# A hand-written list of moves reorders ScalarE, VectorE and GpSimd at the beginning of an attention and gMLP kernel

## The chip, the cores and the metric

The kernel runs as one program on one core of a Trainium2 chip. The core has five engines that each work through their own queue in order: TensorE (PE), VectorE (DVE), ScalarE (ACT), GpSimd (POOL) and SyncE (SP), which here only issues transfers. They wait for each other by semaphores. The metric is the device time of one execution in microseconds (us): 374.2 us, the median of three runs of the kernel before (373.38, 374.2 and 375.71).

## The reference

Two stages follow each other, all in float32. The first is chunked attention with memory: 4 batches, 8 heads, 768 tokens, head dimension 64; each chunk of 32 queries sees 8 memory slots and a window of its own 32 tokens, 16 before and 8 after. The second is a gated MLP with a spatial product.

```python
for c in range(nc):                      # 24 chunks of 32 queries
    k_full = concat([mem_k, k[l_start:r_end]]);  v_full = concat([mem_v, v[l_start:r_end]])
    scores = scale * q_c @ k_full.T
    a = exp(scores - max(scores));  a = a / (sum(a) + 1e-09)
    out[c] = a @ v_full
h = maximum(x @ w_in, 0);  u, v = h[..., :512], h[..., 512:]     # x: (4, 768, 512)
v_n = (v - mean(v)) / sqrt(var(v) + 1e-06)
v_s = einsum('ts,bsd->btd', w_spatial, v_n) + b_spatial
result = (u * v_s) @ w_out
```

## The kernel before, in words

**Tiling and stages.** Attention runs in 24 units of 128 queries (4 chunks of 32, all 8 heads). Each unit goes through: `prep` (ACT copies keys into `kmain`, L400), a burst of 32 small matmuls for the scores (L415, out `sx`), `softmax` (DVE: `top`, a maximum, L472; `sub`, subtract it, L476; ACT: `exp`, L481; DVE: `den`, sum, add, reciprocal, L486 to L489), `flip` (PE transposes the weights into `pt`, L503; ACT copies them to `pT`, L506), a second burst that multiplies by the values (L415, `sx<-vmain,pT`), `norm` (DVE, `xs`, L455), a transpose into `xt` (L519) and the copies to `x` (ACT L524, DVE L528). The values of unit i are written into the second half of the same PSUM tile `sx` that holds the scores of unit i+1. The product with `w_in` (L557 to L559) starts as soon as the first three units and pieces of `w_in` are ready, and is interleaved with the other units. Every float32 product of the second stage is three matmuls of two-part numbers, so each operand is first split.

**Pieces of w_in.** `w_in` arrives as float64 words in eight pieces (`big`, 512 KB each). `from_f64` turns a piece to float32: on ACT `scale_` (L861, into `st`) and `rest` (L866, in place in `big`), on DVE `shift` (two instructions, L870 and L871), on POOL `add` (L876). `split` then makes `high` on ACT (L890, `win_h`) and `low` on DVE or POOL (L894, `win_l`). The first piece is written win(0,1) here; its `low` is on POOL.

**Fillers.** `busy` (L255) gives PE 5, 4, 2, 29 and 1 matmuls on an identity (`idle`), each two records in the profile, between the first units. Nothing reads their result.

**What sets the order.** `Plan.op` collects operations with an engine, a modelled time, what they read and write, and a rank; `Plan.order` makes one list of all of them by modelled start times; `emit` runs through the list and records each operation's instructions. The order of the list is the order of every engine's queue. It also decides the waits: an instruction that touches a tile waits for those recorded ahead of it that wrote that tile, whichever half of the tile they wrote. Transfers on SP wait besides for an earlier transfer's landing (`transfer`), so that a bounded amount is under way.

**Operations that the change and the prediction speak of** (number in the plan, engine, line before): 17 ACT `rest` of win(0,1) L866; 15 ACT `scale_` of it L861; 16 DVE `shift` of it L870, L871; 18 POOL `add` of it L876; 19 ACT `high` of it L890; 20 POOL `low` of it L894; 94 ACT keys of unit 1 L400; 96 PE scores of unit 1; 90 and 100 ACT `exp` of units 0 and 1; 91 DVE `den` of unit 0; 98 and 99 DVE `top` and `sub` of unit 1; 92 and 102 PE transposes `pt` of units 0 and 1; 95 PE values of unit 0, written into unit 1's `sx`; 104 PE transpose `xt` of unit 0; 46 SP load of q for units 2 and 3.

Of the kernel before, what the change touches and what calls it, by code (L numbers as in the profile page):

```python
# [18 lines left out]
CH = 32  # L19
SLOT = 40  # L20
LEFT = 16
FIRST = ('a', 'b', 'w0', 'v0', 'w1', 'w2', 'w3', 'q1', 'v1', 'w4', 'v2', 'w5', 'w6', 'w7')
RANKS = (34.7, 9.5, 12.7, 26.3, 36.3, 2.9, 37.5, 38.2)
LOWS = ('POOL', 'DVE', 'DVE', 'DVE', 'POOL', 'DVE', 'DVE', 'POOL')
# [4 lines left out]
class Plan:  # L29
# [121 lines left out]
        return none  # L151

    def emit(self):
        for n in self.order():
            if n < 0:
                self.idle(-n)
            else:
                self.ops[n][2]()


@with_exitstack
def tile_chunked_attention_gmlp(
# [106 lines left out]
    def src(t, offset, ap):  # L269
        return bass.AP(tensor=t.tensor, offset=offset, ap=ap)  # L270
# [20 lines left out]
    def load(dst, src_, w, rank, r=(), eng="SP", slow=1.0, us=0.45, seq=False, drag=1.0, of=None):  # L291
        e = {"SP": nc.sync, "ACT": nc.scalar, "POOL": nc.gpsimd}[eng]
        n = 4
        for s in src_.shape:
            n *= s
        mb = n / 1e6 * slow
        n = op(eng, us, lambda: transfer(e, dst() if callable(dst) else dst, src_, mb, of), r=r, w=w, rank=rank, mb=mb,
               after=line.get(eng) if seq else None, drag=drag)
        if seq:
            line[eng] = n  # L300
# [10 lines left out]
    def spot(name, g, shape):  # L311
        if (name, g) not in t_:
            alloc(name, g, shape, F32)
        return t_[name, g]

    def load_qk(g, units=(0, 1), seq=True):
# [3 lines left out]
        nk = 2 * UT + CH  # L320
        lo = LEFT if c0 == 0 else 0
        hi = nk - LEFT if c0 + 2 * UC == NC else nk
        q0, q1 = units[0] * UT, units[-1] * UT + UT
# [5 lines left out]
        load(lambda: spot("k", g, [P, T, nk])[:, :, k0:k1],  # L329
             src(k, off - LEFT + k0, [[S, P], [P * S, T], [1, k1 - k0]]), w=[ks + (u,)], rank=10.0 * i, slow=1.15, seq=seq)  # L330

# [55 lines left out]
    def spread_mem(i, eng, rank):  # L387
        b, o = i // UB, (i % NV) * UC
        for r in range(2):
            rows = slice(r * D + CH, r * D + SLOT)  # L390

            def spread(rows=rows, r=r):
                to, of = vmain[rows, :, o:o + UC], memv[rows, b].unsqueeze(2).broadcast_to([M, T, UC, D])
                ins = {"DVE": nc.vector, "POOL": nc.gpsimd}[eng].tensor_copy(to, of)  # L394
                made.setdefault(("vmem", i % NV), []).append(ins.ins.name)
            op(eng, 1.1 if eng == "POOL" else 1.25, spread, r=[("memv", r)], w=[("vmem", i % NV, r)], rank=rank)
# [65 lines left out]
    def softmax(i, rank):  # L462
        c0 = (i % UB) * UC

        def top():
            s = t_["sx", i][:, :, 0]
            if c0 == 0:
                nc.vector.memset(s[0:CH, :, :, 0:LEFT], NEG)
            if c0 + UC == NC:
# [497 lines left out]
    for j in range(NV):  # L967
        spread_mem(j, "DVE" if j < 1 else "POOL", 1.0 + 10 * j)
    for x in FIRST:
        if x[0] == "w":  # L970
# [105 lines left out]
```

## Time and profile before

| what | value |
|---|---|
| median of three runs | 374.2 us |
| the profiled execution | 373.39 us, of which the span of the instructions is 371.6 us |
| PE busy | 356.2 us (96%) |
| DVE, ACT, POOL busy | 294.7, 186.9, 157.1 us |
| first matmul | 6.78 us |
| granted TensorE clock | 1.00 in every slice of the page |

Busy times are shares of the span; an engine's idle time is told with what ended it. A row of a timeline gives start, duration, engine, line and operation; what stands in brackets is the idle time of the engine before it and its releaser. Times are counted from the span's start. The profiled execution took 0.8 us less than the median of the runs.

### The profile page before, as it was taken

How to read it: one execution, taken by the hardware profiler on the slowest of the kernel's cores; microseconds unless marked ns; L12 is line 12 of the kernel's file. 1: busy time of each engine (PE TensorE's matmuls, PEld its weight loads, DVE VectorE, ACT ScalarE, POOL GpSimd, SP SyncE). 2: the span in 40 equal slices, each digit the busy share in tenths (PEclk: the TensorE clock that was granted, in tenths of full speed). 3: DMA queues.
4: the chain of work that ended last, by engine and by line, in shares of the span. 5: the costliest groups of instructions: out<-in, count | busy, mean ns of one | idle time of the engine just before them, and what ended most of it. 6: DMA issues, size and time to landing. Idle time of an engine off the chain costs nothing. (4 is left out here: it accounts for less than half of the span.)

```text
span 371.6 us, 11928 instructions
## 1 busy us (share of the span) xinstructions
PE 356.2 (96%) x5026; PEld 328.6 (88%) x5026; DVE 294.7 (79%) x480; ACT 186.9 (50%) x334; POOL 157.1 (42%) x154
## 2 busy tenths in 40 slices
PE   2899999999999999999999999999999999999995
PEld 2787888988889889889888899989999999999895
DVE  3799968669669499584797689999979896998894
ACT  3577553655555445544483445347434733744451
POOL 6254733366376057720024367851246025216400
PEclk9999999999999999999999999999999999999999
DMA  8998977885895894968743538204830572230015
GB/s 209 291 246 242 233 223 244 260 249 164 251 241 179 217 276 136 266 159 272 222 168 101 215 132 308 94 1 155 228 129 2 196 227 88 85 130 0 0 44 170
DMA packets 47557, 65.52 MB, mean 176 GB/s; under 512 B 4496, under 2 KB 38928, under 8 KB 47504
## 3 DMA queue, kind: packets, MB, share of 16 engines
q1 hardware_dynamic: 46848, 64.44, 58.1%
q8 instruction: 39, 0.64, 0.8%
q10 hardware_dynamic: 656, 0.33, 0.3%
q14 instruction: 14, 0.11, 0.1%
HBM read 45.88 MB, written 18.87 MB: 174 GB/s over the span
## 5 line engine op out<-in xcount | busy, mean ns | idle before, releaser
L707 PE MATMUL y<-wsp,op 128*128 128x384 f32 x288 | 52.4, 337 | 0.0
L761 POOL TENSOR_TENSOR ug<-st,ug 128x384 f32<-128x384 f32 x24 | 34.5, 1453 | 40.1 <-DVE st L753 35.6
L707 PEld LDWEIGHTS y<-wsp,op 128*128 128x128 f32 x288 | 49.9, 188 | 0.4 <-ACT st L747 0.3
L557 PE MATMUL f<-x,win_h 128*128 128x384 f32 x128 | 46.0, 359 | 0.2 <-issue 0.2
L559 PE MATMUL f<-x,win_h 128*128 128x384 f32 x128 | 43.2, 338 | 0.0
L558 PE MATMUL f<-x,win_l 128*128 128x384 f32 x128 | 43.2, 337 | 0.0
L557 PE MATMUL f<-win_h,x 128*128 128x512 f32 x96 | 41.1, 428 | 0.0
L707 PE MATMUL f<-wsp,op 128*128 128x384 f32 x216 | 39.7, 337 | 0.0
L687 DVE TENSOR_TENSOR op<-sm,op 128x768 fp32r<-128x768 f32 x32 | 36.6, 1144 | 2.0 <-ACT op L684 1.8
L558 PE MATMUL f<-win_h,x 128*128 128x512 f32 x96 | 37.9, 395 | 0.1
L707 PEld LDWEIGHTS f<-wsp,op 128*128 128x128 f32 x216 | 37.5, 188 | 0.3 <-DVE st L753 0.3
L559 PE MATMUL f<-win_l,x 128*128 128x512 f32 x96 | 37.7, 393 | 0.0
L707 PE MATMUL y<-wout,op 128*128 128x256 f32 x288 | 36.0, 281 | 0.9 <-DVE op L687 0.8
L455 DVE TENSOR_TENSOR xs<-sx,rec 128x512 f32<-128x512 f32 x24 | 16.6, 690 | 24.6 <-PE sx L415 24.4
L707 PEld LDWEIGHTS y<-wout,op 128*128 128x128 f32 x288 | 34.6, 188 | 1.6 <-DVE op L687 1.5
L593 POOL TENSOR_TENSOR rstd<-ve,mhalf 128x1 f32<-128x1 f32 x24 | 14.5, 604 | 49.0 <-DVE ve L589 47.1
L684 ACT CAST op<-sm 128x768 fp32r<-128x768 f32 x32 | 26.4, 836 | 16.5 <-DVE sm L670 16.4
L767 POOL TENSOR_TENSOR st<-st,bias 128x384 f32<-128x384 f32 x14 | 17.9, 1286 | 38.3 <-ACT st L747 28.7
L415 PEld LDWEIGHTS sx<-kmain,q 64*32 64x32 f32 x1536 | 17.3, 109 | 14.3 <-issue 12.9
L581 ACT ACTIVATE st<-f 128x512 f32<-128x512 f32 x24 | 14.4, 599 | 28.7 <-PE f L559 28.2
L415 PE MATMUL sx<-kmain,q 64*32 64x64 f32 x1536 | 21.3, 230 | 7.4 <-ACT kmain L400 6.8
L394 POOL COPY vmain<-memv 8x1024 f32<-8x1024 f32 x22 | 23.9, 1090 | 9.9 <-PE sx L415 7.7
(86 smaller groups left out, 780.9 us busy)
## 6 DMA issues: line engine op xcount, KB each, us to landing
vmain<-in_v_dram SPq DMA_DIRECT2D x48, 128.0 KB
u_far<-uo SPq DMA_DIRECT2D x32, 192.0 KB
vn_far<-st SPq DMA_DIRECT2D x24, 256.0 KB
vr<-vn_far SPq DMA_DIRECT2D x8, 768.0 KB
ug<-u_far SPq DMA_DIRECT2D x16, 384.0 KB
q<-in_q_dram SPq DMA_DIRECT2D x11, 512.0 KB
vmain<-in_v_dram SPq DMA_DIRECT2D x47, 96.0 KB
out_dram<-ot SPq DMA_DIRECT2D x33, 128.0 KB
```

The costliest lines, as they stand in the source:

```text
L394: ins = {"DVE": nc.vector, "POOL": nc.gpsimd}[eng].tensor_copy(to, of)
L415: ins = nc.tensor.matmul(o, w_, m, start=True, stop=True, skip_group_check=True)
L455: nc.vector.tensor_tensor(xs.rearrange("p t r d -> p r t d"), t_["sx", i][:, :, 1], rec.rearrange("p t r -> p r t").unsqueeze(3).broadcast ...
L557: nc.tensor.matmul(o, lh, rh, start=(j == 0), stop=False)
L558: nc.tensor.matmul(o, ll, rh, start=False, stop=False)
L559: nc.tensor.matmul(o, lh, rl, start=False, stop=(j == len(pairs) - 1))
L593: nc.gpsimd.tensor_tensor(a, t_["ve", i], mhalf, op=ALU.pow)
L684: nc.scalar.copy(half(0), of())
L687: nc.vector.tensor_tensor(half(1), of(), half(0).bitcast(F32), op=ALU.subtract)
L707: nc.tensor.matmul(o, x, y, start=first and m == 1, stop=m == 3 * chunks, skip_group_check=True)
L761: nc.gpsimd.tensor_tensor(g, t_[st(x)], g, op=ALU.mult)
L767: {"DVE": nc.vector, "POOL": nc.gpsimd}[eng].tensor_tensor(a, a, bias[:, 1], op=ALU.add)
```

## The change

A table of pairs (n, m) is applied to the plan's list: operation n is taken out and put right behind operation m. A second table says behind which PE operation how many fillers stand. The 48 pairs touch operations that run in the first 50 us. PE's queue and SP's queue come out with the same instructions in the same order as before, fillers included.

```diff
+MOVES = (
+    (17, 25), (19, 18), (98, 46), (91, 98), (99, 26), (100, 99), (97, 102), (103, 35), (101, 34), (105, 101),
+    ...
+)
+IDLES = ((87, 5), (92, 4), (95, 2), (104, 29), (132, 1))
...
     def emit(self):
-        for n in self.order():
-            if n < 0:
-                self.idle(-n)
-            else:
-                self.ops[n][2]()
+        order = [n for n in self.order() if n >= 0]
+        for n, m in MOVES:
+            order.remove(n)
+            order.insert(order.index(m) + 1, n)
+        idles = dict(IDLES)
+        for n in order:
+            self.ops[n][2]()
+            if n in idles:
+                self.idle(idles[n])
```

Lines behind the table stand 8 to 12 lower in the changed kernel (L400 becomes L412, L866 becomes L878).

**ScalarE, the first unit's part, before.** `p_228` and `p_323` are the weights of units 0 and 1, `big_169` and `st_266` the first piece of `w_in`:

```order
L400 COPY kmain0_147<-k_163 128x20x32
L400 COPY kmain1_148<-k_163 128x20x32
L481 ACTIVATE p_228<-p_228 128x512
L861 ACTIVATE st_266<-big_169 128x512
L866 ACTIVATE big_169<-big_169 128x512
L506 COPY pT_287<-pt_273 128x512
L481 ACTIVATE p_323<-p_323 128x512
L861 ACTIVATE st_333<-big_215 128x512
```

**ScalarE, the same place now** (`p_229`, `p_331`: units 0 and 1; `big_169`, `st_267`: the first piece):

```order
L412 COPY kmain0_147<-k_163 128x20x32
L878 ACTIVATE big_169<-big_169 128x512
L412 COPY kmain1_148<-k_163 128x20x32
L493 ACTIVATE p_229<-p_229 128x512
L873 ACTIVATE st_267<-big_169 128x512
L518 COPY pT_280<-pt_269 128x512
L902 CAST win_h_108<-st_267 128x512
L873 ACTIVATE st_329<-big_220 128x512
L493 ACTIVATE p_331<-p_331 128x512
```

The `rest` of the first piece now stands ahead of the keys of unit 1, and the `high` of the first piece ahead of the `exp` of unit 1.

**VectorE, from the `sub` of unit 0 to that of unit 1, before** (`sx_230`: scores of unit 1, later values of unit 0):

```order
L476 TENSOR_TENSOR p_228<-sx_182,mx_224 128x2x4x64
L486 TENSOR_REDUCE den_268<-p_228 128x8
L487 TENSOR_TENSOR den_268<-den_268,eps_103 128x8
L489 RECIPROCAL rec_271<-den_268 128x8
L472 TENSOR_REDUCE mx_285<-sx_230 128x8
L870 TENSOR_SCALAR st_266<-st_266 128x512
L871 SCALAR_TENSOR_TENSOR st_266<-big_169,st_266 128x512
L476 TENSOR_TENSOR p_323<-sx_230,mx_285 128x2x4x64
```

**VectorE, the same place now** (`sx_231`: the tile that was `sx_230`):

```order
L488 TENSOR_TENSOR p_229<-sx_182,mx_225 128x2x4x64
L882 TENSOR_SCALAR st_267<-st_267 128x512
L883 SCALAR_TENSOR_TENSOR st_267<-big_169,st_267 128x512
L484 TENSOR_REDUCE mx_322<-sx_231 128x8
L498 TENSOR_REDUCE den_324<-p_229 128x8
L499 TENSOR_TENSOR den_324<-den_324,eps_103 128x8
L501 RECIPROCAL rec_327<-den_324 128x8
L488 TENSOR_TENSOR p_331<-sx_231,mx_322 128x2x4x64
```

The same operations stand between the two `sub`; the `shift` comes first, then `top` of unit 1, then `den` of unit 0. In the list of all engines `top` of unit 1 (98) now stands behind operation 46, and so behind the burst 95 that writes into the tile it reads; before, it stood ahead of that burst.

**GpSimd, behind the four copies of memory values, before:**

```order
L876 TENSOR_TENSOR st_266<-st_266,big_169 128x512
L876 TENSOR_TENSOR st_333<-st_333,big_215 128x512
L876 TENSOR_TENSOR st_391<-st_391,big_264 128x512
L894 TENSOR_TENSOR win_l_109<-st_266,win_h_108 128x512
L876 TENSOR_TENSOR st_400<-st_400,big_278 128x512
```

**GpSimd, the same place now:**

```order
L888 TENSOR_TENSOR st_267<-st_267,big_169 128x512
L906 TENSOR_TENSOR win_l_109<-st_267,win_h_108 128x512
L888 TENSOR_TENSOR st_329<-st_329,big_220 128x512
L888 TENSOR_TENSOR st_381<-st_381,big_265 128x512
L888 TENSOR_TENSOR st_398<-st_398,big_278 128x512
```

The `low` of the first piece moved up from fourth to second place.

## Rows read from the trace of the kernel before

**Rows 1.** Waits of PE, 0 to 60 us: total us, times, longest.
```profile
PE sx L415 <- ACT kmain L400: 6.8, 1, 6.8
PE pt L503 <- ACT p L481: 0.9, 1, 0.9
PE pt L503 <- issue: 0.8, 1, 0.8
PE sx L415 <- issue: 0.6, 1, 0.6
```

**Rows 2.** Busy times by stretch: stretch, length, then PE, PEld, DVE, ACT, POOL.
```profile
49.00:371.60 322.60, 316.86 (x4199) 294.74 (x4199) 256.02 (x409) 157.12 (x283) 131.04 (x121) 1.00 0.53 166
```

**Rows 3.** Timeline of PE, 7 to 43 us.
```profile
7.88 2.50 PE L255 MATMUL idle<-ident 128*128 128x128 f32 x10
10.31 1.07 PE L415 MATMUL sx<-kmain,q 64*32 64x64 f32 x64
...
11.80 1.06 PE L255 MATMUL idle<-ident 128*128 128x128 f32 x8
12.79 0.86 PE L415 MATMUL sx<-vmain,pT 64*32 64x64 f32 x64
13.57 0.71 PE L255 MATMUL idle<-ident 128*128 128x128 f32 x4
15.18 0.44 PE L503 MATMUL pt<-ident,p 128*128 128x128 f32 x2 [0.89 <-ACT p L481]
16.37 0.38 PE L503 MATMUL pt<-ident,p 128*128 128x128 f32 x2 [0.75 <-issue]
...
17.02 6.64 PE L255 MATMUL idle<-ident 128*128 128x128 f32 x58
...
42.82 0.85 PE L415 MATMUL sx<-kmain,q 64*32 64x64 f32 x64
```

**Rows 4.** Waits of SP's queue, 7.6 to 10.2 us: total us, times, longest.
```profile
SPq L284 <- DMA big<-in_moe_w_in_dram: 2.2, 1, 2.2
```

**Rows 5.** Timeline of SP, 7.6 to 10.3 us.
```profile
9.79 0.35 SPq L284 DMA_DIRECT2D big<-in_moe_w_in_dram  x1
```

**Rows 6.** Timeline of ACT, 7 to 11 us.
```profile
7.92 0.73 ACT L400 COPY kmain<-k 128x640 f32<-128x640 f32 x1 [1.24 <-DMA k<-in_k_dram]
...
10.23 0.66 ACT L861 ACTIVATE st<-big 128x512 f32<-128x512 f32 x1
10.79 0.67 ACT L866 ACTIVATE big<-big 128x512 uint32<-128x512 uint32 x1
```

**Rows 7.** Timeline of DVE, 10 to 14 us.
```profile
10.35 0.69 DVE L486 TENSOR_REDUCE den<-p 128x8 f32<-128x512 f32 x1 [0.69 <-ACT p L481]
11.07 0.17 DVE L487 TENSOR_TENSOR den<-den,eps 128x8 f32<-128x8 f32 x1
...
11.46 0.69 DVE L472 TENSOR_REDUCE mx<-sx 128x8 f32<-128x512 f32 x1
12.07 0.42 DVE L870 TENSOR_SCALAR st<-st 128x512 uint32<-128x512 uint32 x1
12.52 0.69 DVE L871 SCALAR_TENSOR_TENSOR st<-big,st 128x512 uint32<-128x512 uint32 x1
13.71 0.69 DVE L476 TENSOR_TENSOR p<-sx,mx 128x512 f32<-128x512 f32 x1 [0.49 <-PE sx L415]
```

**Rows 8.** Timeline of POOL, 12 to 40 us.
```profile
13.46 1.28 POOL L876 TENSOR_TENSOR st<-st,big 128x512 uint32<-128x512 uint32 x1 [3.87 <-DVE st L871]
...
37.91 1.31 POOL L876 TENSOR_TENSOR st<-st,big 128x512 uint32<-128x512 uint32 x1 [1.66 <-ACT big L866]
```

**Rows 9.** Timeline of DVE, 38 to 43 us.
```profile
38.41 0.84 DVE L487 TENSOR_TENSOR den<-den,eps 128x8 f32<-128x8 f32 x1
...
42.03 0.68 DVE L455 TENSOR_TENSOR xs<-sx,rec 128x512 f32<-128x512 f32 x1
```

**Rows 10.** Busy times, from the `sub` of unit 1 to the `norm` of unit 3.
```profile
13.71:42.03 28.32, 26.08 (x459) 22.35 (x460) 25.89 (x45) 21.14 (x37) 13.94 (x13) 1.00 0.99 255
```

4 rows, old and new, of the table MOVES are left out of this document.

## The prediction

> **What bounds the kernel now.** I first looked at the busy times: PE works 356.2 of 371.6 us, so an order of the other engines can only matter through PE's pauses. The list of PE's waits up to 60 us [rows 1] shows all that there is before that: 6.8 us until the first keys are there, 0.9 us on an `exp`, and 0.8 and 0.6 us of "issue", in which PE waited for nothing that the profile shows. Behind 49 us PE is busy 316.86 of 322.60 us [rows 2], so a delay that PE carries past there stays to the end: nothing can swallow it.
>
> PE's timeline [rows 3] shows what the reader must see next: between 7.88 and 23.6 us PE is mostly doing fillers. They are a fixed 6.64 us (the last block) that nobody needs, but they stand in PE's queue ahead of real work. So whatever delays the transposes at 15.18 us delays the 29 fillers, and behind them everything. PE's start in this stretch is a chain: keys of unit 1, scores of unit 1 (10.31), values of unit 0 (12.79), DVE's `sub` of unit 1 (13.71, which waited for those values [rows 7]), `exp`, transposes (15.18), fillers (17.02). The change touches exactly the operations of ACT and DVE on this chain.
>
> **The change part by part.** Nothing is added or removed; PE and SP keep their queues, so no transfer is issued in another order. I follow the chain in the new order.
>
> (a) *`rest` ahead of the keys of unit 1.* ACT works in order, so the keys now wait until the first piece of `w_in` has landed. When is that? SP's queue waited 2.2 us for that landing [rows 4] and issued its next transfer at 9.79 us [rows 5]. So `rest` starts at 9.8 instead of finding its data ready. On ACT the next instruction starts 0.56 us behind such an operation (10.23 to 10.79 [rows 6]), so the keys run from 10.4 to 11.1; before they began at 7.92 with 0.73 us. PE had the scores of unit 1 at 10.31, behind fillers that cover the keys; now they start at about 11.2. **+0.9 us**, and the values of unit 0, with the same work between, move from 12.79 to 13.7 and end, with 0.86 us, at 14.55.
>
> (b) *`top` and `den` behind the values burst.* Before, three of DVE's steps (`den` of unit 0, `top` of unit 1, `shift`) ran from 10.35 to 13.2 while PE was still at fillers and values, and only `sub` waited for the values (0.49 us idle [rows 7]). Now `top` of unit 1 is recorded behind the burst that writes into its tile, so it waits for that burst, and `den` of unit 0 stands behind `top`. Work that was hidden comes onto the chain: `top`, 0.61 to 0.72 us by the distance of such reductions to their successors (11.46 to 12.07, 10.35 to 11.07), and `den`, 1.11 us (10.35 to 11.46). `top` starts at 14.6, the sum of `den` at 15.3, its addition of a constant (L487) at 16.05.
>
> (c) *A collision of that addition with POOL.* It took 0.17 us at 11.07 with POOL idle [rows 7], but 0.84 us at 38.41 [rows 9], ending at 39.25, while POOL's addition ran from 37.91 to 39.22 [rows 8]. So it seems to wait for POOL to end. What does POOL do at 16.05 now? `scale_` on ACT stands behind `rest`, the keys and the `exp` of unit 0: it starts 11.5 and ends 12.2. `shift` takes 1.14 us (12.07 to 13.21): 13.35. POOL's `add` begins 0.25 us later (13.46) and takes 1.28 us: 14.9. `high` on ACT, priced like its neighbours at 0.66 us: 15.55. Then POOL's `low`, priced like `add`: 15.55 to 16.85. The addition of `den` at 16.05 falls into it. I take the collision: it ends at 16.9, `sub` starts at 17.1. Without it `sub` would start at 16.3. The margin is half a microsecond on either side, so I keep both.
>
> (d) *To the fillers.* From `sub` to the transposes it was 1.47 us (13.71 to 15.18): 18.6. `norm` of unit 0 fits in that time. Eight transposes at 0.11 us (0.44 for four records, as 16.37 to 17.02 less the pipeline's tail): fillers from 19.45 instead of 17.02. The pause of 0.75 us "issue" in the middle of the old transposes [rows 3] I price at nothing, since PE now stands still for 3.4 us just before (from about 15.2 to 18.6), and whatever brought the instructions late has that time; if it comes back, 0.75 us more. So the fillers start **2.4 us later**; bounds 1.6 (no collision) and 3.2 (pause kept).
>
> (e) *What is recovered up to 49 us.* PE ran from 17.02 to 49 with one unexplained pause, 0.6 us [rows 1]; if that vanishes, 1.8 us are left. The other check is DVE. At `sub` of unit 1 DVE has done the same operations in both orders, and is 3.4 us late (13.71 to 17.1). From there to `norm` of unit 3 at 42.03, which frees the tile for PE's burst at 42.82 [rows 3, 9], the sets are the same again, and DVE was idle 28.32 less 25.89, 2.4 us [rows 10]. If it used all of its idle time it would be 1.0 us late there, and if none, 3.4 us. PE alone says 1.8 to 2.4, DVE 1.0 to 3.4 with a middle of 2.2; the later of the two decides. I take **+2.0 us**. The remaining moves reorder operations inside this stretch; they are hidden behind PE's fillers and products as far as DVE has idle time, and what they cost or give lies within these ends.
>
> (f) *PE's clock over the pause.* The fillers show PE's rate: ten records in 2.43 us (7.88 to 10.31), 0.24 us each, then 58 in 6.64 us, 0.114 us each; the two levels are 1.2 and 2.4 GHz, and the granted clock, told as 1.00 throughout, does not show the lower one there. The pauses of 0.9 and 0.75 us before 17.02 left the fast spacing in place. No row shows a pause of 3.4 us. The sum goes by the rows: nothing for the clock. The Trainium skill ("TensorE: Matmul & The Clock Gate", the section "What's actually happening") says that the slow clock is the default, that sustained work releases it and idling brings it back. By that rule the pause could cost the fast clock, and the sum would be 4.1 instead of 2.0 us, by the price under the second rival.
>
> **The sum.** 373.39 (the profiled execution) + 2.0 = 375.4 us. That execution lay 0.8 us under the median of the runs; a median is forecast, so 374.2 + 2.0 = **376.2 us**. A measurement here tells about 1% (3.7 us) from no change: this is inside.
>
> **The rivals.**
>
> *First: a gain.* The pauses of 0.9, 0.75 and 0.6 us go, PE does the same work: 374.2 less 2.25 = 372.0 us. For it: the `high` and `low` of the first piece come earlier, DVE was busy 25.89 of 28.32 us and a better order there could help. Against: the chain (a) to (d) has no early part; it would need the first piece of `w_in` to land by 8 us, 1.8 before what rows 4 and 5 say. Chance 0.07.
>
> *Second, and on the other side: the clock falls in the pause.* Its place is 15.2 to 18.6 us, the point from which it decides is the length of PE's pause. At the start PE, working from 6.8 us, changed to the fast spacing only between the scores at 10.31 and the fillers at 11.80, so it was slow for 3.5 to 5 us. If it falls back, 4.2 us at half rate are 2.1 us lost, all in front of real work: 374.2 + 4.1 = 378.3 us, over 1% slower. For it: the pause is almost four times the longest one that the rows show. Against: short pauses did nothing. Chance 0.20.
>
> *Third: most is swallowed.* The collision of (c) does not happen (fillers +1.6) and the pause of 0.6 us goes: +1.0 us, and with fewer collisions between DVE and POOL later DVE does not stand in the way: 375.2 us and less, to 374.8. Chance 0.18. For it: (c) rests on a margin of half a microsecond.
>
> The forecast itself, +1.0 to +3.4 around +2.0, has 0.55. That the change would not do what it says is no case: the queues show the moves.
>
> **How the numbers follow.** The range leaves out most of the first rival and the far end of the second, with the runs' own spread: 373.0 to 378.8 us. Faster by over 1% (under 370.5) is not even reached by the first rival: 0.02. Slower by over 1% (over 377.9) holds most of the second rival (0.14) and the upper end of the forecast (0.05): 0.19. Within 1%: 0.79.
>
> **What would show it.** In the new profile ACT's `rest` (L878) should start at about 9.8 us with a wait for the transfer, the keys of unit 1 at 10.4; DVE's `top` (L484) of unit 1 should wait for PE until about 14.6; the constant's addition (L499) should take over 0.5 us; PE should have one pause of some 3.4 us ending at about 18.6 on the `exp`; the fillers should start near 19.5 and keep 0.114 us spacing (0.24 if the second rival holds); `norm` of unit 3 and PE's next scores should come some 2 us later than 42.03 and 42.82. I would be wrong if PE's pause is under a microsecond, if the lag at 42.8 us is gone, or if PE shows new waits behind 49 us.

## The result and the profile after

The changed kernel takes **378.06 us** (median of 22 runs, 375.58 to 382.85), the kernel before beside it 374.72 us (22 runs). The ratio is 1.0078, 95% interval 1.0056 to 1.0099: slower, by just under 1%. The forecast was 376.2 us, range 373.0 to 378.8: the sign, the class (within 1%) and the range held (it took in most of the second rival), but the number is 1.9 us too low, and the time is that of the second rival, 378.3 us, in which TensorE's clock falls.

The profiled execution took 379.64 us (span 377.8), 1.6 us more than the median; before, it was 373.39 (span 371.6). So these two traces are 6.25 us apart, and the runs 3.3.

First, where the difference lies. Busy times by stretch (stretch, length, then PE, PEld, DVE, ACT, POOL), of the changed kernel:

```profile
18.38:48.70 30.32, 26.79 (x455) 23.30 (x456) 24.48 (x46) 19.57 (x35) 10.92 (x10) 0.94 0.93 230
55.00:377.80 322.80, 316.35 (x4199) 294.62 (x4197) 256.87 (x409) 157.14 (x284) 131.08 (x121) 1.00 0.53 166
```

The second row answers to [rows 2]: the same 4,199 matmuls, 322.8 us against 322.6. Over that stretch as a whole nothing is gained or lost. Compared matmul by matmul, PE is 6.6 us late where the kernel before stands at 48 us, 5.4 at 104 us and 6.2 at the end; in between lies an "issue" pause of 0.91 us at 136 us that the kernel before does not have. The 6.2 us are lost ahead of 55 us.

PE's waits up to 65 us of the changed kernel (total us, times, longest):

```profile
PE sx L427 <- ACT kmain L412: 6.9, 1, 6.9
PE sx L427 <- issue: 3.4, 2, 2.1
PE pt L515 <- ACT p L493: 2.5, 1, 2.5
```

And PE's timeline there:

```profile
8.03 2.50 PE L267 MATMUL idle<-ident 128*128 128x128 f32 x10
11.81 1.17 PE L427 MATMUL sx<-kmain,q 64*32 64x64 f32 x64 [1.28 <-issue]
12.91 1.11 PE L515 MATMUL pt<-ident,p 128*128 128x128 f32 x4
13.81 1.91 PE L267 MATMUL idle<-ident 128*128 128x128 f32 x8
15.66 1.02 PE L427 MATMUL sx<-vmain,pT 64*32 64x64 f32 x64
16.60 0.71 PE L267 MATMUL idle<-ident 128*128 128x128 f32 x4
19.79 1.11 PE L515 MATMUL pt<-ident,p 128*128 128x128 f32 x4 [2.48 <-ACT p L493]
20.70 1.06 PE L531 MATMUL xt<-ident,xs 128*128 128x128 f32 x4
21.55 7.29 PE L267 MATMUL idle<-ident 128*128 128x128 f32 x58
...
34.42 0.68 PE L427 MATMUL sx<-kmain,q 64*32 64x64 f32 x42
37.21 0.42 PE L427 MATMUL sx<-kmain,q 64*32 64x64 f32 x22 [2.11 <-issue]
```

Read beside [rows 3], this gives PE's lag step by step. It is 1.5 us at the scores of unit 1 (11.81 against 10.31), 2.9 at the values (15.66 against 12.79), because eight filler records now take 1.91 instead of 1.06 us and four transpose records 1.11 instead of 0.66: PE is still at the slow spacing there. It is 4.6 at the transposes (19.79 against 15.18) and 4.5 at the fillers, although the transposes and the fillers' first records are slow again. The burst of 42 and 22 has an old pause of 0.60 us, which is 2.11 now.

PE's granted clock in that stretch (length, PE busy, clock, share and rate of transfers), of the changed kernel:

```profile
15.00:19.00 4.00, 2.31 (x72) 1.00 0.95 314
19.00:20.00 1.00, 0.21 (x1) 0.74 1.07 334
20.00:22.00 2.00, 2.00 (x11) 0.50 1.12 223
22.00:23.00 1.00, 1.00 (x7) 0.55 1.02 187
23.00:24.00 1.00, 1.00 (x12) 1.00 0.85 189
```

While PE stood still (17.3 to 19.8) the clock fell to the lower level, 1.2 GHz, and it came back only at about 22.9. (The 1.00 of the first row is told although PE ran at the slow spacing until about 16.) Before, it stayed at the upper level, 2.4 GHz, through the pauses of [rows 3].

ACT, then DVE, then POOL, in the same stretch of the changed kernel:

```profile
10.44 0.65 ACT L878 ACTIVATE big<-big 128x512 uint32<-128x512 uint32 x1 [3.61 <-DMA big<-in_moe_w_in_dram]
11.00 0.71 ACT L412 COPY kmain<-k 128x640 f32<-128x640 f32 x1
...
15.54 0.62 ACT L902 CAST win_h<-st 128x512 fp32r<-128x512 f32 x1 [0.90 <-POOL st L888]
16.07 0.68 ACT L873 ACTIVATE st<-big 128x512 f32<-128x512 f32 x1
19.11 0.63 ACT L493 ACTIVATE p<-p 128x512 f32<-128x512 f32 x1 [2.37 <-DVE p L488]
```
```profile
16.74 0.69 DVE L484 TENSOR_REDUCE mx<-sx 128x8 f32<-128x512 f32 x1 [2.75 <-PE sx L427]
17.34 0.68 DVE L498 TENSOR_REDUCE den<-p 128x8 f32<-128x512 f32 x1
18.05 0.17 DVE L499 TENSOR_TENSOR den<-den,eps 128x8 f32<-128x8 f32 x1
18.26 0.20 DVE L501 RECIPROCAL rec<-den 128x8 f32<-128x8 f32 x1
18.38 0.64 DVE L488 TENSOR_TENSOR p<-sx,mx 128x512 f32<-128x512 f32 x1
```
```profile
16.24 1.27 POOL L906 TENSOR_TENSOR win_l<-st,win_h 128x512 fp32r<-128x512 f32 x1 [0.73 <-ACT win_h L902]
```

These answer to [rows 6 to 8]. `rest` waits for its transfer, the keys of unit 1 stand behind it and end at 11.71, and PE starts their scores 0.10 us later: the "issue" in front of 11.81 is this wait under another name. (In e5 and e9 below, which have this move too, it is the same 0.10 us: 11.43 and 11.53, 11.50 and 11.60.) `top` waits for PE, `den` follows, and only then comes `sub`. The addition of `den` took 0.17 us: POOL's `low` had ended at 17.51.

**The clock over all runs.** Each run has its mean granted clock. It counts from the first stretch at the upper level, so a late start is not in it, but a later fall is (0.995 in the profiled run). Where in a run the clock fell it does not say: in the traces of the change, e1 and e2 it fell in the pause in front of the transposes (from 19.5, 18.8 and 17.5 us on), in e3 and e8 only from 184 and 185 us on. Of 22 runs of the change 18 are below 0.998, of 87 runs of the kernel before, beside the experiments, 19. Runs at 0.998 and above are called "full clock" below. Of the change these have a median of 376.2 us (4 runs), the others 378.6; before, beside the first four experiments, 374.0 (22 runs) and 377.4 (7). So at full clock the change costs 2.2 us (95% by resampling the runs 1.2 to 3.1), near the forecast's 2.0; the rest, 1.1 us of the 3.3, goes with the falls.

### The profile page after: what moved, and what is told of

Same layout as the page of the kernel before. It is cut to its first block, busy times and chain, and to the rows that moved or that the text cites. A ratio compares the mean times of both kernels' runs of the same rounds, so it can differ in the third digit from the quotient of the medians.

```text
span 377.8 us, 11929 instructions
## 1 busy us (share of the span) xinstructions
PE 358.6 (95%) x5026; PEld 331.3 (88%) x5026; DVE 293.3 (78%) x480; ACT 185.9 (49%) x334; POOL 156.5 (41%) x154
## 5 line engine op out<-in xcount | busy, mean ns | idle before, releaser
L427 PEld LDWEIGHTS sx<-kmain,q 64*32 64x32 f32 x1536 | 17.3, 109 | 17.2 <-issue 15.8
L427 PE MATMUL sx<-kmain,q 64*32 64x64 f32 x1536 | 21.5, 231 | 10.3 <-ACT kmain L412 6.9
L719 PE MATMUL f<-wout,op 128*128 128x256 f32 x216 | 27.1, 279 | 0.7 <-DVE op L699 0.7
```

Source lines behind the costliest of these rows:

```text
L427: ins = nc.tensor.matmul(o, w_, m, start=True, stop=True, skip_group_check=True)
L719: nc.tensor.matmul(o, x, y, start=first and m == 1, stop=m == 3 * chunks, skip_group_check=True)
```

## The experiments

All were timed in five rounds beside the kernel before, whose medians were 374.66 us (e1 to e4), 374.07 (e5 to e8) and 374.81 (e9 to e12). The theory (A in the texts below): the chain (a) and (b) makes PE pause, and the pause costs the clock. The rivals: the loss sits in the other 44 pairs (B), it is waiting alone, or fillers in the pause do harm themselves (C), or it comes from the supply of instructions to PE (D). In the tables, "full" is the median at full clock less that of the kernel before beside it, with the number of runs.

**Taking steps out of the change.** Four kernels lack some of the four pairs at the front; the other 44 stay.

```diff
-    (17, 25), (19, 18), (98, 46), (91, 98), (99, 26), ...
+              (19, 18), (98, 46), (91, 98), (99, 26), ...   # e1_rest_back
+    (17, 25), (19, 18),                     (99, 26), ...   # e2_top_back
+              (19, 18),                     (99, 26), ...   # e4_chain_back
+                                            (99, 26), ...   # e6_front_back
```

> The change without its first pair: ACT's rest of the first piece of w_in stands behind the exp of unit 0 again, the keys of unit 1 ahead of it. Theory A (the time is lost on the chain up to the 29 fillers, and by TensorE's clock in the pause that this chain makes): scores of unit 1 start at 10.3 us again, the fillers about 1 us earlier than with the whole change, the pause shrinks by 1 us, and the median falls by 1 to 2.5 us from 378.1, to 375.6 to 377. Rival B (the time is lost later, in the moves between 20 and 50 us that crowd VectorE): 377.5 to 378.5.

> The change without the pairs (98, 46) and (91, 98): DVE's den of unit 0 and top of unit 1 stand ahead of the values burst again; rest stays ahead of the keys. Theory A: DVE's sub of unit 1 follows the values at once, but the exp of unit 1 now stands behind the high of the first piece, so the transposes come about 1.5 us earlier than with the whole change; median 375.5 to 377. Rival B: 377.5 to 378.5.

> The change without (17, 25), (98, 46) and (91, 98): the two steps that the prediction prices are undone, the other 45 pairs stay. Theory A: nearly all of the loss goes; what stays is the high of the first piece ahead of the exp of unit 1, up to 1 us: 374.5 to 375.8. Rival B: 377 us or more, since the later moves are all there.

> The change without (17, 25), (19, 18), (98, 46) and (91, 98): also the high of the first piece goes back behind the exp of unit 1, so nothing of the chain up to the 29 fillers is delayed; 44 pairs stay. Theory A: PE's pause in front of the transposes of unit 1 is 1 us as in the kernel before, fillers start at about 17 us, and the time is that of the kernel before, 373.5 to 375. Rival B (the later moves cost too): 376 us or more.

| kernel | median | ratio to before, 95% | full | below 0.998 |
|---|---|---|---|---|
| the change | 378.06 | 1.0078 [1.0056, 1.0099] | +2.2 (4) | 18 of 22 |
| e1, no `rest` | 375.83 | 1.002 [0.9979, 1.006] | +0.1 (2) | 10 of 12 |
| e2, no `top`, `den` | 376.02 | 1.0029 [0.9997, 1.0061] | +1.1 (8) | 4 of 12 |
| e4, only `high` | 376.01 | 1.0034 [1.0002, 1.0067] | +1.1 (4) | 8 of 12 |
| e6, none of the four | 373.76 | 1.0008 [0.9975, 1.0042] | -0.1 (9) | 3 of 12 |

e6 settles the place: with the 44 pairs alone the time is that of the kernel before (interval -0.9 to +1.6 us), so the loss comes with the four. Taking out either half of the chain gives back 2 us of the 3.3. But e4, with both out, is no better than e1 or e2. Its ACT timeline shows one reason:

```profile
14.98 0.62 ACT L902 CAST win_h<-st 128x512 fp32r<-128x512 f32 x1 [1.73 <-POOL st L888]
15.51 0.66 ACT L873 ACTIVATE st<-big 128x512 f32<-128x512 f32 x1
16.07 0.61 ACT L493 ACTIVATE p<-p 128x512 f32<-128x512 f32 x1
```

`high` waits 1.73 us for POOL, and the `exp` of unit 1, now behind it, starts at 16.07 although `sub` (14.55, 0.69 us) had ended at 15.2. This is pair (19, 18), which the prediction did not price. It makes the long block of fillers 0.65 us late in e4 (17.67 against 17.02). By 31 us this lag is gone, as the old pause of 0.60 us does not come in this trace; its later lag, 1.7 us at the end, comes with other "issue" pauses (1.18 us at 50.6). So what the pair costs e4 is open. In the changed kernel it costs nothing: `high` is done at 16.2 and ACT stands idle 2.37 us before that `exp`. In their waits the steps hide behind each other, so their prices do not add.

PE in e1 (timeline, then clock as above):

```profile
17.62 0.66 PE L515 MATMUL pt<-ident,p 128*128 128x128 f32 x4 [2.75 <-ACT p L493]
...
18.54 8.27 PE L267 MATMUL idle<-ident 128*128 128x128 f32 x58
```
```profile
19.00:22.00 3.00, 3.00 (x16) 0.50 1.00 202
```

After a pause of 2.75 us the clock fell, and the 58 filler records took 8.27 instead of 6.64 us [rows 3].

**One step alone, in the kernel before.**

```diff
+MOVES = ((17, 25),)                                             # e9_only_rest
+MOVES = ((98, 46), (91, 98), (99, 91), (97, 99), (100, 99))     # e10_only_top
```

> The kernel before with one move alone: `rest` of the first piece ahead of the keys of unit 1. Chain theory, step (a): keys of unit 1 start at 10.4 to 11.0 instead of 7.92, values of unit 0 end 0.9 to 1.6 us later, the transposes of unit 1 wait 1.8 to 2.5 us for the `exp`, and at full clock the time is 0.5 to 1.2 us over the kernel before (374.2 to 375.2 where it has 374.0). If the clock falls with a pause of that length, most runs show a mean clock below 0.998 and the median is 376 to 377. Rival, by which step (a) was covered by the work on VectorE (`den`, `top` and `shift` ran until 13.2): the pause stays at about 0.9 to 1.5 us and the time within 0.3 us of the kernel before.

> The kernel before with step (b) alone: `top` of unit 1 and `den` of unit 0 behind the burst of values of unit 0, `sub` of unit 1 behind them. Chain theory: `top` waits until about 13.7, `sub` starts near 15.5 instead of 13.71, the transposes wait about 2.7 us instead of 0.89, and the time at full clock is 0.8 to 1.8 us over the kernel before (374.8 to 375.8). With a pause as long as that the clock theory expects a mean clock below 0.998 in more than half of the runs and a median of 376 to 377.5. Rival (the time comes from `rest` and `high` on ScalarE alone): within 0.3 us of the kernel before.

| kernel | median | ratio, 95% | full | below 0.998 |
|---|---|---|---|---|
| e9 | 375.98 | 1.0006 [0.9973, 1.004] | +1.8 (10) | 2 of 12 |
| e10 | 375.37 | 1.0011 [0.9976, 1.0046] | +1.2 (8) | 4 of 12 |

By the ratios neither is told from the kernel before; at full clock both are slower (95% +0.6 to +2.3 and +0.1 to +2.0). PE's timeline of e9 and of e10:

```profile
11.60 1.17 PE L421 MATMUL sx<-kmain,q 64*32 64x64 f32 x64 [1.19 <-issue]
...
13.61 1.91 PE L261 MATMUL idle<-ident 128*128 128x128 f32 x8
...
17.94 0.66 PE L509 MATMUL pt<-ident,p 128*128 128x128 f32 x4 [0.89 <-ACT p L487]
...
18.87 6.64 PE L261 MATMUL idle<-ident 128*128 128x128 f32 x58
```
```profile
12.45 1.06 PE L261 MATMUL idle<-ident 128*128 128x128 f32 x8
...
17.41 0.66 PE L509 MATMUL pt<-ident,p 128*128 128x128 f32 x4 [2.48 <-ACT p L487]
...
18.34 6.64 PE L261 MATMUL idle<-ident 128*128 128x128 f32 x58
```

In e9 the pause at the transposes stayed as before (0.89 us; the chain theory had 1.8 to 2.5); its trace shows the wait for the keys and, behind it, a **late start of the upper level**: the fillers still run at 0.24 us a record. The long block starts 1.85 us later, beside +1.8 in the medians at full clock (this execution's span is 2.6 us longer). In e10 the start was early, and the lag at the long block, 1.3 us, is near the +1.2 at full clock. But its pause of 2.48 us, as long as the change's, was followed by no fall here, and only 4 of 12 runs are below 0.998, beside 7 of 29 of the kernel before: expected was over half. Nor do pause and falls go together over the kernels: e2's trace has a pause of 2.75 us at 4 of 12 runs, e4's one of 1.61 at 8 of 12. A long pause alone does not decide it; what else does stays open.

**Filling the pause.** Twelve fillers are put behind the values of unit 0, in e3 beyond the others, in e5 taken from the long block.

```diff
-IDLES = ((87, 5), (92, 4), (95, 2), (104, 29), (132, 1))
+IDLES = ((87, 5), (92, 4), (95, 14), (104, 29), (132, 1))   # e3_fill_pause
+IDLES = ((87, 5), (92, 4), (95, 14), (104, 17), (132, 1))   # e5_fill_moved
```

> The change with 12 more fillers (14 instead of 2) in front of the transposes of unit 1, in PE's pause of 2.5 to 3.4 us; nothing else is moved. Theory A with the clock: 12 fillers take 2.7 us at the fast spacing, fit into the pause and keep the fast clock, so the median falls by about 2 us, to 376.2, and the mean granted clock of all runs is 1.00. Rival C (the clock costs little, all of the loss is waiting): 378 us, or up to 380 if the fillers are run at the slow spacing of 0.43 us and end behind the exp.

> The change, with 12 of the 29 fillers moved into PE's pause (14 in front of the transposes of unit 1, 17 behind); PE has as many instructions as before, and from the first product on they lie at the same places of its stream. Theory A with the clock: PE is not idle long enough to lose the fast clock, and the block in front of the first product is 2.7 us shorter, so the fillers end up to 2.7 us earlier: 374 to 376 us, mean clock 0.998 or more in most runs. Theory D (twelve more fillers cost 4.8 us in the run before because of PE's instruction supply: the pauses that the profile calls issue come where a block of the stream is used up, and any shift of the stream moves them): here the stream is not shifted behind 24 us, so there is no such loss. Rival C (fillers in the pause are bad in themselves): 380 us or more.

e5: 375.73 us, ratio 1.0038 [1.0006, 1.007], 3 of 12 runs below 0.998, against 18 of 22: with the pause filled the clock stays in most runs. Beside the kernel before, e5 loses 1.7 us and the change 3.3, so about 1.7 are back, though the intervals of the ratios overlap. At full clock e5 is at +1.9 us (9 runs) and the change at +2.2, so what came back is the clock and not the waiting. e3 missed its forecast (376.2 us and a clock of 1.00): 382.84 us, 1.021 [1.0167, 1.0253], all six runs below 0.998. Its timeline shows that the pause was not filled but moved:

```profile
17.98 2.61 PE L267 MATMUL idle<-ident 128*128 128x128 f32 x21 [2.36 <-issue]
```

In e5 the pause at this place was 0.28 us. The clock did not fall here: the 21 records behind the pause took 2.61 us, in e5 too. In this trace it fell from 184 us on, which is taken up below. In e3 DVE's constant addition also met POOL, started at 16.03 beside POOL's `low` (15.98 to 17.25) and took 1.25 us.

**More and fewer fillers in the kernel before.** e3's pause lies in the middle of fillers, which wait for nothing. Three kernels shift PE's stream of instructions (no moves), and a fourth is e6 with the shift of e11.

```diff
+    self.idle(11)   # e7_prewarm: ahead of the first burst; 0 behind it, 23 in the long block
+    self.idle(12)   # e8_more_front: ahead of the first burst, beyond the others
-    ... (104, 29) ...
+    ... (104, 25) ...   # e11_fewer; e12_back_fewer: the same, with the 44 pairs
```

> The kernel before (no moves) with fillers laid otherwise, 41 as before: 11 ahead of the first burst, where PE waits for the keys anyway, none behind it, 23 instead of 29 in the long block. Clock part of theory A: PE reaches the fast spacing before or at the first burst, the scores of unit 1 start at 8.8 instead of 10.3 us, the long block is 1.3 us shorter; up to 1.5 us are gained where the transfers allow it: 372.5 to 374. Rival (the chain through DVE and the landing of keys for units 2 and 3 at 21 us sets the start of the first product): 374.7, no change.

> The kernel before (no moves) with 12 more fillers ahead of the first burst, where PE waits for the keys until 6.8 us; all else is the same, so they cost no time of their own, but every later PE instruction lies 12 fillers further in PE's instruction stream. Theory D: the issue pauses come at other places, and the time changes by 1 us or more, up or down, with more issue time in the list of PE's waits. Without D: 374.7 or a little less, since the first burst runs at the fast spacing.

> The kernel before with 25 instead of 29 fillers in the long block; nothing else. Four fillers are eight records of 0.114 us, 0.9 us. By the chain alone the time is 0 to 0.9 us less (373.1 to 374.0 at full clock), less the more of it VectorE lets through. By the theory of the instruction stream, every later instruction of TensorE stands four fillers further up, and the pauses of 'issue' fall elsewhere: then the time may be off by more than 1 us in either direction, and rows of 'issue' over 1 us stand at other bursts than in the kernel before.

> The 44 pairs without the four of the first chain, and 25 instead of 29 fillers in the long block. The 44 pairs alone gave 373.6 at full clock, the same as the kernel before. By the chain alone this gives 372.7 to 373.6; by the theory of the instruction stream it differs from its twin without the 44 pairs by less than 0.5 us, since TensorE's queue is the same in both, and both may be off by over 1 us.

| kernel | median | ratio, 95% | full | below 0.998 |
|---|---|---|---|---|
| e7 | 375.17 | 1.0037 [1.0012, 1.0062] | | 12 of 12 |
| e8 | 380.2 | 1.0126 [1.007, 1.0182] | | 6 of 6 |
| e11 | 380.74 | 1.0112 [1.0058, 1.0165] | +4.1 (2) | 4 of 6 |
| e12 | 378.25 | 1.007 [1.0028, 1.0113] | +1.9 (6) | 6 of 12 |

Twelve fillers more and four fewer both cost about 6 us, so it is not their work. e7 missed its forecast of 372.5 to 374 us: in its trace the clock rose at 7.1 us already, but fell at 10.5, behind a wait of 1.97 us for POOL, and at 17.4, behind the pause shown below. PE's bursts with pauses, in the kernel before, in e11, in e8 and in e7:

```profile
29.21 0.67 PE L415 MATMUL sx<-kmain,q 64*32 64x64 f32 x42
30.49 0.42 PE L415 MATMUL sx<-kmain,q 64*32 64x64 f32 x22 [0.60 <-issue]
```
```profile
29.39 0.74 PE L421 MATMUL sx<-kmain,q 64*32 64x64 f32 x50
31.68 0.34 PE L421 MATMUL sx<-kmain,q 64*32 64x64 f32 x14 [1.55 <-issue]
```
```profile
15.11 0.38 PE L423 MATMUL sx<-vmain,pT 64*32 64x64 f32 x18 [1.45 <-issue]
```
```profile
14.10 0.80 PE L423 MATMUL sx<-vmain,pT 64*32 64x64 f32 x58 [0.61 <-DMA vmain<-in_v_dram]
16.82 0.31 PE L423 MATMUL sx<-vmain,pT 64*32 64x64 f32 x6 [1.92 <-issue]
```

These early pauses are the smaller part of the loss. Against the same matmul in the kernel before, e8 is 1.4 us late where that kernel stands at 48 us, 5.0 at 168 and 9.7 at 182; e11 is 1.2 us late at 63 us, 3.0 at 79, 2.1 at 154 and 4.2 at 168. In between lie more pauses of the same kind, and in e8 TensorE's clock fell right behind the longest (timeline, then clock as above; below them PE's waits of e11 from 49 us on):

```profile
184.81 0.34 PE L423 MATMUL sx<-vmain,pT 64*32 64x64 f32 x13 [2.04 <-issue]
```
```profile
186.00:187.00 1.00, 1.00 (x4) 0.50 0.63 172
```
```profile
PE sx L421 <- issue: 3.4, 2, 1.8
```

e3 has the same twelve fillers more. It pauses at the same matmul, the 3,511th, for 2.06 us, and its clock fell there too; so its six runs below 0.998 are no evidence on the pause that it was to fill.

The counts give it away. Four fillers are eight records; without them the same burst is cut at 50 instead of 42. In records from the start of the program the cut is at the 475th both times, in the changed kernel too. The pause of 0.75 us in [rows 3] is at the 221st; in e7 and e8 it is at the 221st again, which is now inside a burst of values, and in e3 and e5 at the 222nd, among the fillers. So **these pauses belong to a place in PE's stream, not to the work there**. The page of the changed kernel lists (queue, kind: packets, MB, share)

```profile
q8 instruction: 39, 0.64, 0.7%
```

which are 16 KB each, one for about 129 of PE's 5,026 matmuls and their loads; the 221st and the 475th are two such pieces apart. The later pauses stand on the same grid: the 1,360th (e11, e12), 1,866th (e3), 3,005th (e11) and 3,511th (e3, e8) lie 7, 11, 20 and 24 times about 126.5 records behind the 475th. In the trace's transfer records the packet nearest ahead of such a pause ended 1.3 to 1.5 us before PE went on (before: 15.10 and 16.37, 29.06 and 30.49; the change: 35.71 and 37.21; e8: 13.78 and 15.11; e11: 30.38 and 31.68). That PE waits there for its own instructions fits all of this; why a packet comes late in one program and in time in another stays open. e12 was expected within 0.5 us of e11 and came out 2.2 us lower at full clock (with two runs of e11): it too pauses at the 1,360th, 2.14 us, but not at the 475th or the 3,005th. So TensorE's queue alone does not fix the price. No kernel here beats the one before; e6 equals it.

## Why the prediction was right or wrong

**What bounds the kernel: right.** Behind 55 us the stretch kept its length (322.8 against 322.6 us), and PE's lag of 6.6 us at 48 us is 6.2 at the end.

**(a) Right, its consequence missed.** `rest` waited for its transfer and the keys for it. PE's scores of unit 1 came 1.5 us later, not 0.9, as the transfer landed 0.7 us later than in the trace before. What (a) did not see: PE now stands still for 1.1 to 1.3 us while it is still at the lower level, and in three of the five profiled kernels with this move (the change, e5, e9) the upper level came only at 15.7 to 16.3 us. In the two others (e2, e3), and in all profiled kernels without the move but e7 and e8, whose starts have more fillers, it came between 10.1 and 12.8; in e2 and e3 that was at the start of the pause or just ahead of it (10.7 and 10.1). The late start is worth 1.4 us in the rows above, and e9 has it without a fall. That the pause delays the upper level is read from these traces; no run tested it.

**(b) Right.** `top` waited until the values had ended, with `den` behind it, and the transposes had one pause (2.48 us; forecast 3.4, as the values before it ended late).

**(c) Wrong in the trace of the change, right in others.** The margin of half a microsecond was the point: with a late clock the addition starts 2.0 us later than forecast, POOL's `low` only 0.7. Where the clock starts early, the addition meets POOL (e3 1.25 us; e1 0.44 us). So late clock and collision stand in for each other.

**(d) Mis-sized.** The fillers start 4.5 us later, not 2.4: +0.6 from the transfer and +1.4 from the late start in (a), +0.9 from the half clock in the transposes (19.79 to 21.55, forecast 0.85), and 0.8 less without the collision (`top` to `sub` 1.64 us instead of 2.5). The old pause of 0.75 us went, as forecast: the packet of its place ended at 16.62, well ahead of the `exp`.

**(e) Wrong in this execution.** Nothing was recovered up to `norm` of unit 3: it came at 48.70, 6.7 us late [rows 9], since PE added 0.65 us of slow fillers and the pause of 2.11 us. DVE had 5.8 idle us in the stretch, against 2.4 [rows 10]; it was not what held PE. Over the runs at full clock the +2.0 us of the forecast stands beside +2.2. That is partly luck: the sum holds a collision of 0.8 us that this trace lacks, and lacks the late start of 1.4; what the runs at full clock are made of was not profiled.

**(f) The step that failed.** It priced the clock at nothing, because the pauses of 0.9 and 0.75 us had left it up. The second rival named the place, the pause, and a price of 2.1 us; measured are 2.4 us between the medians of the change's runs with and without a fall, and in its trace 1.6 (0.9 in the transposes, 0.65 in the fillers). It got 0.20; 18 of 22 runs have a fall, and in the profiled one it lies in the pause. What one profiled execution at 1.00 could not show: the kernel before itself loses the clock in 19 of 87 runs; where, no trace shows. The rule quoted there (the Trainium skill, "TensorE: Matmul & The Clock Gate", section "What's actually happening") thus was the better guide here; the traces of the change, e1 and e2 agree, and those of e10 (2.48 us) and e3 (2.36 us), with pauses as long and no fall behind them, do not. The same section says that the point at which the clock rises at the start varies from run to run, as it depends on when the first matmul comes. The traces without the move agree that it varies: apart from e7 and e8, it lies between 10.9 and 12.8 us, with first matmuls at 6.7 to 7.2. Whether something like it decides which pause is followed by a fall is not shown.

**The unpriced pair (19, 18)** cost nothing beside the others; when they are gone it delays the fillers by 0.65 us (e4). The remaining 44 pairs cost nothing that e6 could tell, as the prediction had it.

## What to carry to other kernels

A short wait on TensorE near its start is not worth its own length: it can delay the upper clock or bring the lower one back, here 1.4 us in three of five traces for a wait of 1.2, and 1.6 to 2.4 in most of the change's runs for one of 2.5. Moves that delay one chain hide each other, so price them together and take them out one by one. And an instruction that does no harm in time still shifts the stream behind it: change the number of fillers only with a measurement, or keep it and move them, as e5 did.

## What the runs showed of the hardware that was not expected

- The clock fell in or behind pauses of 1.8 to 2.8 us in some traces (the change, e1, e2, e7; e3 and e8 at 184 us) and not in others with pauses as long (e10 2.48 us, e12 2.14, e11 1.82).
- PE pauses at fixed places of its instruction stream (its 221st and 475th matmul records), for 0.28 to 2.36 us, and at more places on the same grid later. Two kernels with twelve fillers more (e3, e8) both stood still for 2 us at the 3,511th record and lost the clock there; four fewer moved the pauses to other places of it. Either costs about 6 us.
